# Moving small TensorE work behind the P V bursts, and dealing the score maxima by a table, in a fused attention and mixture-of-experts kernel

## The chip, the cores and the metric

One program on one core of a Trainium2 chip. The metric is device time in microseconds (us). The kernel before has a median of 1517.07 us over 3 runs (1515.82 to 1519.51). The engines of the core work through their own queues in order and wait for one another by semaphores: TensorE (PE in the profile; its weight loads are listed as PEld), VectorE (DVE), ScalarE (ACT), GpSimd (POOL) and SyncE (SP, which issues most DMAs).

## The reference

Attention with pooled queries over 8 batches of 8 heads (1152 keys of 64 values, neighbouring queries averaged to 576), and on its rows a top-1 mixture of 8 experts.

```python
q_pool = q.reshape(B, H, S // 2, 2, D).mean(axis=3)
scores = scale * np.matmul(q_pool, k.transpose(0, 1, 3, 2))
scores = scores - np.max(scores, axis=-1, keepdims=True)
attn = np.exp(scores)
attn = attn / (np.sum(attn, axis=-1, keepdims=True) + 1e-09)
x = np.matmul(attn, v)                       # then rows (batch, query), 512 columns
...
logits = x @ w_gate                          # 8 experts
e_idx = np.argmax(logits, axis=1)
probs = np.exp(logits - logits.max(-1, keepdims=True)); probs /= probs.sum(-1, keepdims=True) + 1e-09
eom = 1.0 / (1.0 + np.exp(-(x @ w_output_gate)))
for e in range(E):
    mask = e_idx == e
    h = np.maximum(x[mask] @ w1[e], 0.0)
    out[mask] = gate_w[mask, None] * eom[mask, e, None] * (h @ w2[e])
```

## The kernel before

**Pairs and steps.** Two heads make a pair; there are 32 pairs, four to a batch. `attention` works in steps, 18 to a pair: one step for each of the 9 blocks of 128 keys of each of the two heads. Below, "step 14" is the place of a step within its pair, counted from 0. The whole order of TensorE, VectorE, ScalarE and GpSimd is the order of the Python loop over `s` (`tc.manual_schedule`, lines 640 to 691); only SyncE's DMAs are ordered by the framework. One step issues, in this order: what was put off in the step before (`sends`, `pendv`), routers, one piece of `fill`, the scores of the step, preparations of later pairs (`prep_at`), maxima, transposes of maxima (`rows`), and a burst of P V.

**Scores** (`scores`, lines 383 to 412). Four matmuls (lines 393 and 395) write one of two score buffers `sps` in PSUM; the buffers alternate from step to step. ScalarE reads it twice, for a high half `ph` in 16 bits and for the full exponent. In the six steps of `PLP` (1, 3, 7, 9, 11 and 13) the second exponent is written back to the PSUM buffer (lines 399 and 400) and VectorE subtracts the two for the low half `pl` (line 403, called `lo`); this subtraction is put off to the start of the next step. In the other twelve steps GpSimd subtracts (line 409).

**Maxima** (`mgen`, lines 308 to 341). The greatest score of each query is found one pair ahead: 27 units to a pair, 9 query tiles by 3 blocks of 384 keys. A unit is two matmuls into a PSUM bank `mp` (line 330; three for tile 4) and one reduction on VectorE (line 331). After 15 units (tiles 0 to 4) and after 27 (tiles 5 to 8) a small reduction (line 338) gathers `m9`. `rows` (lines 360 to 381) transposes it on TensorE (line 365), VectorE splits the result in two (lines 370 and 371, in the next step), and `sends` issues two DMAs from ScalarE's queue into rows 66 and 67 of `qb` (line 376), from which the scores of the next pair subtract it. Up to step `s` the number of units is 1.5 times the steps, rounded down: one in even steps, two in odd ones. From the fourth pair on `rows` is called in even steps, ahead of the burst.

**P V bursts** (`av`, lines 414 to 440). A block of keys is 15 matmuls (lines 424 to 426) of 64 or 65 columns; bursts run in even steps alone, six steps behind the scores, in the sizes of `BURST`. The blocks of one head add up in a single PSUM tile `av`. Its last block is in the burst of step 14 (first head) or step 4 (second head). Then `norm` (lines 433 to 435, VectorE) divides, at the next `pop`, and the next head's burst, in step 16 or 6, overwrites the tile.

**Banks.** `psum` (lines 87 to 101) hands out three PSUM banks in turn, the longest unused first. With `hold` a bank stays out of the turn until `free`. Maxima, their transposes (held until split), the row sums `gmax` of step 14 (line 272, held until `scale(1)`, line 279, at the end of that step), and everything of `logits` and `router` use them.

**Logits and router** (lines 470 to 601). When a pair's rows are done, `logits` transposes them to `xh` and `xl` (line 479, in the starts of steps 8 and 10) and multiplies them by the gate weights in two column ranges of 256 and 320 (line 496, two matmuls each, starts of steps 12 and 14). `wgt` has 128 columns, of which 32 carry weights (`WC`, line 48) and the rest zeros. After a batch's fourth pair the generator goes on with `router`, from step 16: transposes of the logits (line 521), some twenty small VectorE operations on a held bank, then again on another, and five indirect DMAs from GpSimd. A generator that yields 1 goes on in the next even step, one that yields nothing in the next step.

After the attention, `Moe` runs the experts; the change doesn't touch it.

Of the kernel before, what the change touches and what calls it, by code (L numbers as in the profile page):

```python
# [19 lines left out]
LEAD = 18  # L20
L0 = 18
LS = 0
# [6 lines left out]
PREP = ((0, 'lk'), (12, 'kh', 0), (12, 'qsum'), (17, 'kh', 1), (18, 'kl'), (18, 'dk', 0), (19, 'dk', 1), (22, 'qh'), (24, 'dq', 0), (25, 'dq', 1), (26, 'ql'), (29, 'qd'), (30, 'dl', 0), (32, 'dl', 1),  # L29
        (63, 'lv'), (82, 'amax', 0), (88, 'amax', 1), (93, 'gmax'), (94, 'scale', 0), (95, 'scale', 1), (99, 'scale', 2), (100, 'vh', 0), (101, 'vs', 0), (103, 'vl', 0), (107, 'vh', 1), (107, 'vs', 1), (110, 'vl', 1))  # L30
BURST = {0: 2, 2: 2, 4: 2, 6: 2, 8: 1, 10: 2, 12: 2, 14: 2, 16: 3}
PLP = (1, 3, 7, 9, 11, 13)
PLPL = (1, 3, 5, 17)
IMM = 0
# [7 lines left out]
TLAG = 1  # L42
# [2 lines left out]
P32 = 6  # L45
SLEAD = 32
S = 1152
WC = 128
NQ = 576
NC = 9  # L50
SHIFT = 4.0 * math.log(2.0)
# [15 lines left out]
def attention(tc, qT, kT, vL, wg, keep, xrows, idscr, cum, pairs, setup, scat, init, exps):  # L67
    nc = tc.nc
    nb = len(pairs) // 4
    with ExitStack() as ctx:  # L70
# [16 lines left out]
        def psum(hold=False, name="tp"):  # L87

            while len(held) == 3:
                pop() if fill else pendv.pop(0)()  # L90
            k = next(i for i in banks if i not in held)
            free(k)
            if hold:
                held.add(k)
            x = ps_m.tile([128, 512], F32, name=name, tag=f"mp{k}")
            return (x, k) if hold else x

        def free(k):
            held.discard(k)
            banks.remove(k)  # L100
            banks.append(k)
# [22 lines left out]
        def dmaf(o, i, q=nc.sync):  # L124
            q.dma_start(out=o.bitcast(F32), in_=i.bitcast(F32))
# [218 lines left out]
        now = [0]  # L344

        def pop(k=1):
            while k and fill:
                fill.pop(0)()
                k -= 1

        pend_t, pendd = [], []

        def sends():

            while pendd and pendd[0][1] < now[0]:
                pendd.pop(0)[0]()
# [1 line left out]
        pendv = []  # L358

        def rows(force=False):  # L360
            while pend_t and (force or now[0] >= pend_t[0][-1] + TLAG):
                m9, nt, t0, t1, qbf, _ = pend_t.pop(0)
                tp, tk = psum(True)
                tp = tp[0:nt, 0:128]
                nc.tensor.transpose(out=tp, in_=m9[:, 0:nt], identity=ident)
                mr = sm.tile([5, 2, 128], F32R, name="mr")[0:nt]
                c0 = 16.0 * SHIFT

                def split(tp=tp, tk=tk, mr=mr, qbf=qbf, t0=t0, t1=t1, nt=nt):
                    nc.vector.tensor_scalar(out=mr[:, 0], in0=tp, scalar1=c0, scalar2=None, op0=ALU.subtract)  # L370
                    nc.vector.scalar_tensor_tensor(out=mr[:, 1], in0=tp, scalar=c0, in1=mr.bitcast(F32)[:, 0], op0=ALU.subtract, op1=ALU.subtract)
                    free(tk)

                    def send():
                        for j in range(2):
                            dmaf(qbf[66 + j:67 + j, 128 * t0:128 * t1].rearrange("o (t n) -> o t n", n=128), mr[:, j], nc.scalar)
                    pendd.append((send, now[0]))
                if now[0] < 18:
                    split()
                else:  # L380
                    pendv.append(split)

        def scores(st, h):
            ka, kb, qa, qb = st['ka'], st['kb'], st['qa'], st['qb']
            o = h * (NQ + 64)
            for c in range(NC):
# [10 lines left out]
                ph2 = ph.rearrange("p (j n) -> p j n", j=2)  # L397
                if c + 9 * h in (PLP if st['n'] < LASTN else PLPL):
                    nc.scalar.activation(out=ph2, in_=x, func=AF.Exp, scale=1.0 / 16)  # L399
# [42 lines left out]
        routers = []  # L442

        wf = bp.tile([128, 4, 16], F32, name="wf")
        wgt = bp.tile([128, 4, WC], F32R, name="wgt")
        em8 = keep['em8']
# [23 lines left out]
        def logits(b, c, xb):  # L470

            xh = sm.tile([128, NQ], F32R, name="xh", bufs=1)
            xl = sm.tile([128, NQ], F32R, name="xl", bufs=1)
            yield 1
            for c0, c1, grp in ((0, 256, (0, 1)), (256, NQ, (2, 3, 4))):
                tx, tk = psum(True)
                for i, t in enumerate(grp):
                    x = xb[:, t, 128 * c:128 * c + 128]
                    nc.tensor.transpose(out=tx[:, 128 * i:128 * i + 128], in_=x, identity=ident)  # L479
                d = 0  # L480
                for o, w in ((0, c1 - c0),) if c0 == 0 else ((0, 256), (320, 64)):
                    z = slice(c0 + d, c0 + d + w)
                    nc.scalar.copy(out=xh[:, z], in_=tx[:, o:o + w])

                    def sub(o=o, w=w, z=z, tx=tx, tk=tk if not d else None):
                        nc.vector.tensor_tensor(out=xl[:, z], in0=tx[:, o:o + w], in1=xh.bitcast(F32)[:, z], op=ALU.subtract)
                        if tk is not None:
                            free(tk)
                    fill.insert(0, sub)
                    d += w  # L490
                yield 1
            for c0, c1 in ((0, 256), (256, NQ)):
                pop(99)
                tl = psum()
                for j, x in enumerate((xh, xl)):
                    nc.tensor.matmul(tl[:, 0:c1 - c0], lhsT=wgt[:, c], rhs=x[:, c0:c1], start=j == 0, stop=j == 1)  # L496
                if c == 0:
                    nc.vector.tensor_copy(out=lT[:, c0:c1], in_=tl[0:32, 0:c1 - c0])
                else:
                    nc.vector.tensor_tensor(out=lT[:, c0:c1], in0=tl[0:32, 0:c1 - c0], in1=lT[:, c0:c1], op=ALU.add)  # L500
                yield 1
            if c == 3:
                yield from router(b, xb)

# [114 lines left out]
        NP = len(pairs)  # L619
        pos = dict(m=0)  # L620

        def adv(k, g, want):
            while pos[k] < want:
                next(g, None)
                pos[k] += 1
# [3 lines left out]
        def prep_at(s, ph):  # L629
            u = 3 * (s + SLEAD) + ph  # L630
            for n in range(max(u // 54 - 2, 0), min(u // 54 + 2, NP)):
                r = u - 54 * n + min(3 * (LEAD - 15), 2 * n)
                if r == 0:
                    preps[n] = prep(n, PREP if n > 1 else PREP0 if n else PREPF)
                if n in preps:
                    for f in preps[n].pop(r, ()):
                        f()

        E = mybir.EngineType
        with tc.manual_schedule(engines={E.PE, E.DVE, E.Activation, E.Pool}):  # L640
            for s in range(-SLEAD, 0):
                for ph in range(3):
                    prep_at(s, ph)
                if s == -RI:
                    for i in (1, 2):
                        dmaf(QBs[i][64:66], QBs[0][64:66])
                        dmaf(KBs[i][64:68], KBs[0][64:68])
                if s == 1 - SLEAD + INIT:
                    consts()
                if s == -3:  # L650
                    init(0)
                if s >= -int(L0):
                    adv('m', mg, int(1.5 * (s + 1 + L0)))
                    now[0] = s
                    sends()
                    pop(3)
                    rows()
            for s in range(18 * NP + 14):
                now[0] = s
                live = s < 18 * NP  # L660
                if s % 18 == 2 and 0 < s // 18 < 5:
                    with tc.issue_after(lastk[0].ins):
                        init(s // 18)
                sends()
                while pendv:
                    pendv.pop(0)()
                for r in routers:
                    if not s % 2 or not live or not r[1]:
                        r[1] = next(r[0], 0)
                pop()  # L670
                if live:
                    next(sg)
                prep_at(s, 0)
                mw = min(27 * NP, int(1.5 * (s + 1 + min(LEAD, L0 + LS * s))))
                if pos['m'] < mw:
                    adv('m', mg, pos['m'] + 1)
                prep_at(s, 1)
                adv('m', mg, mw)
                if s < 54 or s % 2 == 0:
                    rows()  # L680
                if pos['m'] == 27 * NP:
                    pop(2)
                j = s - ALAG
                for _ in range(BURST.get(j % 18, 0) if 0 <= j < 18 * NP else 0):
                    next(ag)
                prep_at(s, 2)
                if not live:
                    pop(3)
            pop(99)
            for r in routers:  # L690
                for _ in r[0]: pass
# [529 lines left out]
```

## Time and profile before

| | |
|---|---|
| runs, median (lowest to highest) | 1517.07 us (1515.82 to 1519.51) |
| the profiled execution | 1520.83 us, span of its instructions 1519.1 us |
| mean granted TensorE clock | 0.988 |
| DVE busy | 1100.6 us (72%) |
| ACT busy | 1119.0 us (74%) |
| POOL busy | 1014.8 us (67%) |
| attention, by the windows view | from about 26 to 1014 us, TensorE busy 971.3 of 988 us |

A row of the timeline gives the start in us from the span's start, the length in us, the engine, the line and operation, the tiles (out<-in) and the shape. Ends of matmuls are modelled, so the time that one matmul costs is read from its start to the next one's start. In the rows of groups, "x" is the number of instructions, then come their busy time in us and the mean of one in ns, then the engine's idle time just before them. In the waits, the three numbers are the total in us, the number of times, and the longest.

### The profile page before, as it was taken

What the parts mean: (1) busy time and instruction counts of PE and PEld (TensorE: products, weight loads), DVE (VectorE), ACT (ScalarE), POOL (GpSimd) and SP (SyncE); (2) the same over time, 40 slices, a digit from 0 to 9 for tenths busy, and PEclk for the clock granted to TensorE, in tenths of its full rate; (3) what the DMA queues carried; (4) which work ended last, traced back from release to release, by engine and by line L of the source; (5) the groups of instructions that cost most, each with busy time, mean ns of one, the idle gap of its engine ahead of it and who ended that gap; (6) DMA issues with size and microseconds to landing.
All of it is one profiled execution on the core that took longest, in us unless ns stands there. A gap on an engine that the chain in (4) does not pass through costs nothing.

```text
span 1519.1 us, 40914 instructions
## 1 busy us (share of the span) xinstructions
PE 1475.8 (97%) x15838; PEld 1344.3 (88%) x15838; DVE 1100.6 (72%) x2359; ACT 1119.0 (74%) x1949; POOL 1014.8 (67%) x892
## 2 busy tenths in 40 slices
PE   7999999999999999999999999988999999999998
PEld 6999999999998999999999899976888888888875
DVE  7677777777786777777678777737877877777752
ACT  5788888888887878888888888884655655655642
POOL 5887888788878879788888988796243333333410
PEclk9999999999999999999999999998999999999999
DMA  5577466665676556656567556357876676367650
GB/s 169 137 189 191 124 167 166 169 155 134 161 170 159 122 135 172 169 145 163 124 165 180 144 149 167 72 202 270 313 251 236 209 238 238 108 228 256 228 194 36
DMA packets 96787, 265.96 MB, mean 175 GB/s; under 512 B 12906, under 2 KB 17146, under 8 KB 96578
## 3 DMA queue, kind: packets, MB, share of 16 engines
q1 hardware_dynamic: 85994, 241.52, 56.7%
q0 software_dynamic: 9152, 20.85, 3.8%
q8 instruction: 129, 2.11, 0.6%
q10 hardware_dynamic: 1440, 0.89, 0.2%
q14 instruction: 72, 0.59, 0.1%
HBM read 164.23 MB, written 23.02 MB: 123 GB/s over the span
## 4 chain that ended last, share of the span: by engine, by line
PE 91%; DVE 4%; ACT 2%; DMA 1%; issue 1%; POOL 1%; ACTq 0%; POOLq 0%; DVEq 0%; SPq 0%
PE mp L330 20%; PE hps L913 14%; PE sps L393 11%; PE sps L395 9%; PE av L424 6%; PE av L425 6%; PE av L426 6%; PE yp L937 4%; PE yp L935 4%; PE yp L936 4%; DVE pm L331 2%; PE yp L933 1%; PE tp L479 1%; PE xps L892 1%; PE tp L496 1%
## 5 line engine op out<-in xcount | busy, mean ns | idle before, releaser
L331 DVE TENSOR_REDUCE pm<-mp 128x1 f32<-128x384 f32 x864 | 452.9, 550 | 225.4 <-PE mp L330 224.4
L409 POOL TENSOR_TENSOR pl<-p,ph 128x576 f16<-128x576 f32 x386 | 494.2, 1286 | 152.8 <-ACT ph L408 122.2
L407 ACT ACTIVATE p<-sps 128x576 f32<-128x576 f32 x386 | 252.8, 655 | 103.1 <-PE sps L395 61.0
L330 PE MATMUL mp<-ka,qa 128*128 128x384 f32 x960 | 315.5, 345 | 0.0
L424 PEld LDWEIGHTS <-ph 128*128 128x128 f16 x2880 | 263.3, 97 | 39.6 <-issue 28.3
L424 PE MATMUL av<-vt,ph 128*128 128x65 f16 x2880 | 296.8, 194 | 0.0
L425 PE MATMUL av<-vt,ph 128*128 128x64 f16 x2880 | 294.8, 195 | 0.0
L426 PE MATMUL av<-vt,pl 128*128 128x65 f16 x2880 | 293.9, 193 | 0.0
L393 PE MATMUL sps<-qa,ka 128*128 128x288 f32 x1152 | 279.5, 324 | 12.7 <-ACT ph L408 8.7
L425 PEld LDWEIGHTS <-ph 128*128 128x128 f16 x2880 | 266.2, 97 | 0.8
L426 PEld LDWEIGHTS <-pl 128*128 128x128 f16 x2880 | 266.4, 99 | 0.0
L330 PE MATMUL mp<-kb,qb 66*128 66x384 f32 x768 | 261.5, 340 | 0.9 <-DVE kb L204 0.6
L408 ACT ACTIVATE ph<-sps 128x576 f16<-128x576 f32 x386 | 251.4, 651 | 0.0
L395 PE MATMUL sps<-qb,kb 68*128 68x288 f32 x1152 | 248.1, 298 | 0.0
L913 PE MATMUL hps<-x,w1h 128*128 128x512 f32 (+2 forms) x704 | 224.9, 384 | 4.2 <-DVE x L897 4.2
L393 PEld LDWEIGHTS sps<-qa,ka 128*128 128x128 f32 x1152 | 185.2, 192 | 17.3 <-ACT ph L408 11.7
L395 PEld LDWEIGHTS sps<-qb,kb 68*128 68x128 f32 x1152 | 186.9, 191 | 0.0
L330 PEld LDWEIGHTS mp<-ka,qa 128*128 128x128 f32 x960 | 179.4, 191 | 1.7 <-DVE pm L331 1.5
L915 ACT COPY hs<-hps 128x512 f32<-128x512 f32 (+2 forms) x88 | 47.4, 538 | 168.2 <-PE hps L913 168.2
L913 PE MATMUL hps<-x,w1l 128*128 128x256 f32 (+2 forms) x704 | 163.5, 273 | 0.0
L403 DVE TENSOR_TENSOR pl<-sps,ph 128x576 f16<-128x576 f32 x190 | 143.6, 756 | 15.7 <-ACT sps L400 14.0
L399 ACT ACTIVATE ph<-sps 128x576 f16<-128x576 f32 x190 | 124.4, 655 | 40.4 <-PE sps L395 31.3
(254 smaller groups left out, 2944.4 us busy)
## 6 DMA issues: line engine op xcount, KB each, us to landing
ka<-xk SPq DMA_DIRECT2D x120, 288.0 KB
raw1b<-in_w_dram SPq DMA_DIRECT2D x24, 1024.0 KB
raw2b<-in_w_dram SPq DMA_DIRECT2D x24, 1024.0 KB
raw1a<-in_w_dram SPq DMA_DIRECT2D x22, 1024.0 KB
raw2a<-in_w_dram SPq DMA_DIRECT2D x22, 1024.0 KB
vp<-in_vL_dram SPq DMA_DIRECT2D x32, 576.0 KB
qp<-in_qT_dram SPq DMA_DIRECT2D x31, 576.0 KB
kpf<-in_kT_dram SPq DMA_DIRECT2D x31, 576.0 KB
```

Of the source, the lines that this page charges most:

```text
L330: nc.tensor.matmul(mp, lhsT=l, rhs=r, start=j == 0, stop=j == len(ops) - 1)
L331: nc.vector.tensor_reduce(out=pm[:, i:i + 1], in_=mp, axis=AX.X, op=ALU.max)
L393: nc.tensor.matmul(sps[:, j, 0:288], lhsT=ka[:, h, ks], rhs=qa[:, o + 288 * j:o + 288 * j + 288], start=True, stop=False)
L395: nc.tensor.matmul(sps[:, j, 0:288], lhsT=kb[:, h, ks], rhs=qb[:, h, 288 * j:288 * j + 288], start=False, stop=True)
L403: nc.vector.tensor_tensor(out=pl.rearrange("p (j n) -> p j n", j=2), in0=x, in1=ph2, op=ALU.subtract)
L407: nc.scalar.activation(out=p32.rearrange("p (j n) -> p j n", j=2), in_=x, func=AF.Exp, scale=1.0 / 16)
L408: e_ = nc.scalar.activation(out=ph2, in_=x, func=AF.Exp, scale=1.0 / 16)
L409: nc.gpsimd.tensor_tensor(out=pl, in0=p32, in1=ph, op=ALU.subtract)
L424: nc.tensor.matmul(av_[:, qb, 0:65], lhsT=hi, rhs=vt[:, h, c, 0:65], start=c == 0 and qb == 0, stop=False)
L425: nc.tensor.matmul(av_[:, qb, 0:64], lhsT=hi, rhs=vt[:, h, c, 66:130], start=False, stop=False)
L426: nc.tensor.matmul(av_[:, qb, 0:65], lhsT=lo, rhs=vt[:, h, c, 0:65], start=False, stop=c == NC - 1 and qb == 4)
L913: nc.tensor.matmul(hp[:, f, 0:n], lhsT=W1[l][g][:, c, fs], rhs=d['x'][:, c, 0:n], start=c == 0 and l == 0, stop=c == 3 and l == 0)
```

## The change

The maxima of a step come from the table `UNITS` instead of the rule of 1.5. Against the rule one unit moves from step 1 to 0, from 11 to 10, from 13 to 12 and from 15 to 14. Transposes of maxima are made behind the burst of an even step (in the first three pairs they can still come ahead of it); those of tiles 0 to 4 are held back by two steps more, from step 12 to 14. `logits` yields 4 after its second transposes and after its first product; the loop turns 4 into 2 behind the burst of an even step and resumes a 2 behind the burst of the next one. So the two gate products move from the starts of steps 12 and 14 to the ends of steps 12 and 16, and the router begins at step 18, which is step 0 of the pair after, not 16. `wgt` has 32 columns, and the products write 32 partitions.

```diff
+UNITS = (2, 1, 1, 2, 1, 2, 1, 2, 1, 2, 2, 1, 2, 1, 2, 1, 1, 2)
...
-WC = 128
+WC = 32
...
-            while pend_t and (force or now[0] >= pend_t[0][-1] + TLAG):
+            while pend_t and (force or now[0] >= pend_t[0][-1] + (TLAG if pend_t[0][2] or now[0] < 54 else TLAG + 2)):
...
-                yield 1
+                yield 1 if c0 == 0 else 4
...
-                    nc.tensor.matmul(tl[:, 0:c1 - c0], lhsT=wgt[:, c], rhs=x[:, c0:c1], start=j == 0, stop=j == 1)
+                    nc.tensor.matmul(tl[0:32, 0:c1 - c0], lhsT=wgt[:, c], rhs=x[:, c0:c1], start=j == 0, stop=j == 1)
...
-                yield 1
+                yield 4 if c0 == 0 else 1
...
-                    if not s % 2 or not live or not r[1]:
+                    if not live or not r[1] or r[1] == 1 and not s % 2:
                         r[1] = next(r[0], 0)
...
-                mw = min(27 * NP, int(1.5 * (s + 1 + min(LEAD, L0 + LS * s))))
+                mw = min(27 * NP, 27 * (s // 18 + 1) + sum(UNITS[:s % 18 + 1]))
...
-                if s < 54 or s % 2 == 0:
+                if s < 54:
                     rows()
...
                     next(ag)
+                if s % 2 == 0:
+                    rows()
+                    for r in routers:
+                        if r[1] == 2:
+                            r[1] = next(r[0], 0)
+                        elif r[1] == 4:
+                            r[1] = 2
```

## The prediction

> **What bounds the kernel now.** I read the page first, then the waits, then the timelines of one ordinary pair (the sixteenth, whose step 13 starts at 515.44 us), engine by engine.
>
> ```profile
> span 1519.1 us, 40914 instructions
> ...
> PE 1475.8 (97%) x15838; PEld 1344.3 (88%) x15838; DVE 1100.6 (72%) x2359; ACT 1119.0 (74%) x1949; POOL 1014.8 (67%) x892
> ...
> PE mp L330 20%; PE hps L913 14%; PE sps L393 11%; PE sps L395 9%; PE av L424 6%; PE av L425 6%; PE av L426 6%; PE yp L937 4%; PE yp L935 4%; PE yp L936 4%; DVE pm L331 2%; PE yp L933 1%; PE tp L479 1%; PE xps L892 1%; PE tp L496 1%
> ```
>
> The chain that ended last is TensorE's own order of work; what the change moves, L330's maxima, stands at its head, and the gate products (L496) are its 1%. TensorE waits for almost nothing, so whatever it is spared counts in full, and so does every new wait.
>
> ```profile
> PEld sps L393 <- ACT ph L408: 11.7, 13, 2.5
> ...
> PEld tp L479 <- DVE pm L331: 5.1, 9, 0.6
> ```
>
> These are its two old waits that matter: scores that wait for ScalarE to clear a score buffer, and transposes that wait 0.57 us each for a bank that VectorE must clear.
>
> ```profile
> 514.25 0.33 PE L330 MATMUL mp<-kb,qb 66*128 66x384 f32 x1
> 514.43 0.27 PE L365 MATMUL tp<-ident,m 128*5 128x128 f32 x1
> 514.54 0.19 PE L424 MATMUL av<-vt,ph 128*128 128x65 f16 x1
> ```
>
> ```profile
> 515.44 0.51 PE L393 MATMUL sps<-qa,ka 128*128 128x288 f32 x2
> ...
> 516.06 0.34 PE L330 MATMUL mp<-ka,qa 128*128 128x384 f32 x1
> ...
> 516.76 0.31 PE L496 MATMUL tp<-xh,wgt 128*128 128x320 f32 x1
> ...
> 517.06 0.42 PE L393 MATMUL sps<-qa,ka 128*128 128x288 f32 x2
> ...
> 517.59 0.28 PE L272 MATMUL tp<-am,onesf 128*128 128x2 f32 x2
> 517.73 0.42 PE L330 MATMUL mp<-ka,qa 128*128 128x384 f32 x1
> 517.99 0.34 PE L330 MATMUL mp<-kb,qb 66*128 66x384 f32 x1
> 518.17 0.21 PE L424 MATMUL av<-vt,ph 128*128 128x65 f16 x1
> ...
> 518.64 0.51 PE L393 MATMUL sps<-qa,ka 128*128 128x288 f32 x2
> ```
>
> Here every instruction starts as soon as the one before has streamed. Scores take 0.53 us (517.06 to 517.59), 0.61 to 0.62 behind a burst (515.44 to 516.06); their first two matmuls last 0.51 instead of 0.42. A unit of maxima takes 0.35 (516.06 to 516.76 are two), a burst of one block 0.47 (518.17 to 518.64).
>
> **The change part by part.**
>
> *Behind the burst, the gain.* The extra 0.08 us of scores behind a burst is a 128-column weight load that the short P V matmuls do not cover: behind the longer gate products the same scores have no such loss. Anything with a light weight load and a long enough stream, put between burst and scores, gets these 0.08 us for nothing.
>
> ```profile
> L496 PEld LDWEIGHTS tp<-xh,wgt 128*128 128x128 f32 x64 | 12.2, 190 | 1.0 <-DVE pm L331 0.6 <-ACT xh L483 0.4
> ...
> L365 PEld LDWEIGHTS tp<-ident,m 128*5 128x5 f32 x32 | 2.8, 87 | 1.0 <-DVE m L338 0.6 <-DVE ri L786 0.4
> ```
>
> A transpose of maxima loads 5 columns (87 ns against 190). Ahead of the burst it costs 0.11 us (514.43 to 514.54), less some 0.01, as a burst starts a little slower without it: 0.10. Behind the burst it costs its 0.11 less the 0.08 it hides: 0.03. That saves 0.07 each for two in each of 28 pairs and one in the fourth: 57 x 0.07 = 4.0 us. The gate products stream as long as before (0.15 us each here); with the full load of 190 ns they would themselves pay the 0.08 behind a burst and gain nothing. A 32-column load isn't in the trace. Between the two rows by columns it would be 87 + 27/123 x 103 = 110 ns, near the lower one, so I take the whole saving, 62 x 0.08 = 5.0 us (two groups in 31 pairs; the last pair's run after the steps). Its bounds are 0 and 5.0. Together -9.0 us, or -4.0.
>
> [...]
>
> *Fewer zeros by themselves.* A 128-column load was hidden behind the product before it (516.76 to 517.06, two products of 0.15, is the stream alone), so unmoved it would gain nothing. VectorE read only 32 partitions before, too.
>
> *The table.* No unit is added. Steps 0, 10, 12 and 14 get two, the steps after them one: TensorE's sum is the same, but step 13 shrinks, from two units and a product (516.06 to 517.06) to one unit, 0.35. Step 14 now asks for four banks: the row sums hold one to the step's end, two units take the other two, and then the transpose must have the first unit's bank back. What clears it stands behind the subtraction of step 13 in VectorE's queue.
>
> ```profile
> 516.80 0.65 ACT L400 ACTIVATE sps<-sps 128x576 f32<-128x576 f32 x1
> 517.27 0.69 ACTq L125 DMA_DIRECT2D qb<-mr  x1
> ```
>
> ```profile
> 515.56 0.27 DVE L370 TENSOR_SCALAR mr<-tp 5x128 fp32r<-5x128 f32 x1
> 515.86 0.28 DVE L371 SCALAR_TENSOR_TENSOR mr<-tp,mr 5x128 fp32r<-5x128 f32 x1
> ...
> 517.55 0.76 DVE L403 TENSOR_TENSOR pl<-sps,ph 128x576 f16<-128x576 f32 x1
> 518.23 0.47 DVE L500 TENSOR_TENSOR lT<-tp,lT 32x320 f32<-32x320 f32 x1
> 518.63 0.54 DVE L331 TENSOR_REDUCE pm<-mp 128x1 f32<-128x384 f32 x1
> 519.09 0.15 DVE L277 TENSOR_SCALAR tp<-tp 128x2 uint32<-128x2 uint32 x1
> 519.27 0.16 DVE L279 TENSOR_SCALAR inv<-tp 128x2 f32<-128x2 f32 x1
> 519.35 0.21 DVE L433 TENSOR_SCALAR r<-av,sc 128x5 f32<-128x5 f32 x1
> ...
> 519.82 0.49 DVE L435 TENSOR_TENSOR xb<-av,r 128x320 f32<-128x320 f32 x1
> ```
>
> I walk both queues from the end of step 13's scores (516.06 above). VectorE: the subtraction starts at +1.49, when ScalarE's second exponent is out (517.45), and leaves after 0.68; the first unit's reduction ends at 2.17 + 0.54 = +2.71. TensorE: one unit 0.35, scores 0.53, row sums with the slower unit behind them 0.22, two units 0.70, the burst 0.47: it is at the transpose at +2.27. **It waits 0.44 us**, or 0.5 with a semaphore's delay. VectorE goes on: the reduction leaves at +2.63, then `scale` 0.18, the second reduction 0.46, `scale` 0.10, the split 0.30 + 0.27, which the transpose has brought here from a step earlier, and `norm` 0.96 (519.35 to 520.31): +4.90. TensorE without any wait would be at the next head's burst in step 16 at 2.27 + 0.11 + 0.53 + 0.35 + 0.53 + 0.35 = +4.14. That burst overwrites the tile which `norm` reads. So the two waits come to **some 0.8 us a pair**, where there were none: now the burst of step 16 comes at 518.64 + 0.61 + 0.70 + 0.53 + 0.35 = 520.83, 0.5 us after `norm`. If the splits queue tighter it is 0.65, with every semaphore's delay 0.95. In 28 pairs, 22.4 us (18.2 to 26.6); in the first three the transpose can stay ahead, and I leave them at nothing.
>
> *The router, two steps later.* Its banks are held in steps 0 to 4 and 6 to 10 of the next pair instead of two steps less. In step 3 two units then find the bank of the maxima's transpose still unsplit, and in step 10 the second transposes meet the router's second bank. Each is like the collision that the trace has in step 8 (0.57 us, above): 2 x 0.57 in 7 pairs, 8.0 us, between 0 (another bank happens to be free) and 12. VectorE's and GpSimd's router work is otherwise the same.
>
> *The DMAs of the maxima,* two per group on ScalarE's queue, come two steps later for tiles 0 to 4.
>
> ```profile
> 735.86 2.82 ACTq L125 DMA_DIRECT2D qb<-mr  x2
> ```
>
> In this pair ScalarE's queue was held for 2.82 us by the two, where an issue is 0.7: an older transfer on the same semaphore had to land first. That is what the 11.7 us of scores waiting for ScalarE mostly are. Three microseconds later those transfers have landed, unless the framework deals the semaphores another way. I take three quarters, -8.8 us, between -11.7 and 0. Queued behind these issues stand step 16's exponents and the value copies; by the walk they lose 0.5 us and TensorE doesn't notice.
>
> *Sum:* 1520.83 - 9.0 + 22.4 + 8.0 - 8.8 = 1533.4 us for an execution like the profiled one. That one was 3.76 us over the median of the runs, so the median comes to **1529.7 us**. With all low ends together it is 1515, with all high ends 1552; the high ones have separate causes and will hardly meet, so I give this case 1515 to 1546.
>
> **The rivals.**
>
> *Faster: VectorE keeps up.* If in step 14 the reduction isn't behind the subtraction, or ScalarE clears step 13 earlier by the 0.8 us, only the gains are left: 1517.07 - 9.0 - 8.8 = 1499 us. For it speaks that VectorE is busy 72% only and that ScalarE loses a queue wait; it decides where the bank is back before +2.27. Against it stands the exponent's end at +1.39, which moves with the scores themselves: a shorter step 13 brings TensorE to the bank sooner and VectorE not at all.
>
> *No change.* The router's collisions don't come, ScalarE's waits all go, and the pair loses 0.65: 1517.07 - 9.0 + 18.2 - 11.7 = 1515 us.
>
> *Column tiles drain the array.* A change of the array's shape is in the trace, at the transposes of logits with 32 rows:
>
> ```profile
> 423.98 0.33 PE L330 MATMUL mp<-kb,qb 66*128 66x384 f32 x1
> 424.25 0.49 PE L521 MATMUL tp<-ident,lT 32*128 32x32 f32 x5
> 424.67 0.53 PE L393 MATMUL sps<-qa,ka 128*128 128x288 f32 x2
> ```
>
> It starts 0.27 us after the maxima's matmul, not 0.18, and five short transposes and the way out take 0.42: some 0.09 in and 0.2 out. If products of 32 columns did that, 62 groups would lose 0.29 each, 18 us: 1548 us. Against it: transposes with 5 columns (514.43) come and go without a gap. [...]
>
> *The maxima come too late.* Their second DMA is issued at 517.27 in step 14, for the scores of the next pair's step 0. These come one step 15 (1.31 us), one step 16 (1.82) and one step 17 (1.31) after 518.64, at 523.1 by the costs above, so it has 5.8 us now and, two steps (2 x 1.4) later, 3.0. If landing took 4, TensorE would lose 1.0 us in 28 pairs: 1558 us. No row gives its landing; that it moves 2.5 KB speaks against it.
>
> *The table does nothing*, because `mw` is already met: not so, the running sums differ in steps 0, 10, 12 and 14.
>
> **How the numbers follow.** Forecast 0.58 (0.06 of it at its low end, within the bound), faster 0.18, no change 0.12, drain 0.05, late maxima 0.07. A measurement of this kernel can tell 0.3%, 4.6 us. Slower: 0.52 + 0.05 + 0.07 = 0.64; the same: 0.06 + 0.12 = 0.18; faster: 0.18. The likeliest case alone spans 1515 to 1546; the range must reach into the faster one and takes 1508 to 1546, leaving out about 0.10 below and 0.09 above.
>
> **What would show it.** Right: in the waits, rows of L365 for the reductions of L331 and of L424 for L435, each some 28 times and 0.4 us; scores behind a moved transpose or product with 0.42 instead of 0.51; the queue's 2.82 us gone; pairs of some 30.6 us, and TensorE's busy share lower. Wrong: no wait at the transposes of step 14; a gap before L496 of 0.1 us or more (drain); L395 waiting for a DMA in step 0; or a time below 1512 us, which would mean that VectorE's order of step 14 isn't the one I walked.

## The result, and the profile after

After: 1613.35 us median of 6 runs (1609.15 to 1615.17), beside 1516.88 us of 6 runs of the kernel before; the ratio is 1.0628 (95% interval 1.0609 to 1.0647). The change costs 96.5 us. The forecast was slower, by 12.8 us.

The head of the page, with the chain that ended last (line numbers of after are one higher than before up to the burst, later by more):

```profile
span 1613.0 us, 40820 instructions
...
PE 1516.1 (94%) x15838; PEld 1359.7 (84%) x15838; DVE 1109.0 (69%) x2359; ACT 1111.6 (69%) x1949; POOL 1018.3 (63%) x892
...
PE 75%; DMA 10%; DVE 6%; issue 3%; ACT 3%; POOL 2%; SPq 0%; ACTq 0%; POOLq 0%; DVEq 0%
PE mp L331 15%; PE hps L921 14%; PE sps L394 8%; PE sps L396 8%; DMA qb<-mr 8%; PE av L425 5%; PE av L426 4%; PE av L427 4%; PE yp L945 4%; PE yp L943 4%; PE yp L944 4%; DVE pm L332 2%; DVE pl L404 2%; DMA qa<-yq 1%; PE yp L941 1%
```

TensorE's share fell from 97% to 94%, and a transfer that wasn't on the chain at all, the maxima's DMA into `qb`, now holds 8% of it. The waits name who stands behind it (total in us, times, longest):

```profile
PE sps L396 <- DMA qb<-mr: 50.3, 23, 5.1
PE tp L366 <- DVE pm L332: 8.7, 27, 0.4
...
PEld sps L396 <- DMA qb<-mr: 52.8, 22, 5.3
PEld tp L366 <- DVE pm L332: 12.0, 27, 0.5
PEld L425 <- DVE xb L436: 7.1, 29, 0.3
```

The waits of L366 (the transposes of maxima in step 14) and of L425 (the burst of step 16) were forecast; that of L396 (the scores of step 0, for the maxima's DMA) was the rival with a chance of 0.07. Read from each start to the next, it is 54.0 us in 23 pairs: 4.2 to 5.3 us in step 0 of the third pair of a batch (pairs 6, 10, 14, 18, 22 and 26 from 0), 0.7 to 2.2 in 17 others. The timeline shows both kinds, first an ordinary pair (steps 14 to 0), then a third one:

```profile
529.36 0.55 DVE L332 TENSOR_REDUCE pm<-mp 128x1 f32<-128x384 f32 x1
...
529.97 0.28 PE L366 MATMUL tp<-ident,m 128*5 128x128 f32 x1 [0.31 <-DVE pm L332]
...
530.00 0.51 PE L394 MATMUL sps<-qa,ka 128*128 128x288 f32 x2
...
531.67 0.69 ACTq L126 DMA_DIRECT2D qb<-mr  x1
...
532.87 0.31 PE L497 MATMUL tp<-xh,wgt 128*32 128x320 f32 x1
...
533.02 0.31 PE L497 MATMUL tp<-xl,wgt 128*32 128x320 f32 x1
...
533.17 0.43 PE L394 MATMUL sps<-qa,ka 128*128 128x288 f32 x2
...
534.40 0.43 PE L394 MATMUL sps<-qa,ka 128*128 128x288 f32 x2
...
535.60 0.30 PEld L396 LDWEIGHTS sps<-qb,kb 68*128 68x128 f32 x2 [1.00 <-DMA qb<-mr]
...
766.29 0.53 SPq L576 DMA_DIRECT2D xrows<-xb  x1
...
767.36 0.66 SPq L577 DMA_DIRECT2D xrows<-xb  x1
...
768.06 1.52 SPq L152 DMA_DIRECT2D kpf<-in_kT_dram  x1
...
770.18 1.41 ACTq L126 DMA_DIRECT2D qb<-mr  x1
...
778.24 0.82 PE L396 MATMUL sps<-qb,kb 68*128 68x288 f32 x2 [4.83 <-DMA qb<-mr]
```

In step 14 the transpose (529.97) starts when the reduction of 529.36 has cleared its bank. The second DMA is issued at 531.67; the weights of the scores that need it could load at 534.60 (535.60 less the 1.00 us waited): 3.9 us from issue to use, 2.9 on hand. In the third pair, where the same 2.5 KB take 8.0 us, SyncE had issued the batch's rows (1.2 MB, L576 and L577) and the next keys (L152, 0.6 MB) 2.1 to 3.9 us ahead of them. The gate products also show what was hoped for: 0.15 us each (532.87, 533.02, 533.17), no gap ahead, and scores of 0.43 behind them.

What follows such a wait is in the windows view (stretch, length, busy time of PE, PEld, DVE, ACT and POOL, granted clock, DMA share, GB/s):

```profile
773.00:776.60 3.60, 0.41 (x3) 0.18 (x2) 0.93 (x3) 1.57 (x3) 3.58 (x5) 1.00 1.11 194
776.60:780.00 3.40, 1.76 (x6) 1.62 (x6) 0.26 (x1) 0.84 (x2) 0.86 (x1) 0.51 0.19 73
780.00:783.40 3.40, 3.40 (x38) 3.26 (x37) 0.85 (x2) 1.25 (x3) 2.82 (x3) 0.50 0.00 0
783.40:786.80 3.40, 3.40 (x48) 3.23 (x47) 2.56 (x6) 2.71 (x6) 2.73 (x3) 0.99 0.28 66
```

TensorE stands still for most of the first stretch, and in the next two its clock is halved: a second loss, after the wait. The trace has 81.9 us at half clock within the attention, 20.5 before (10.2 us of each are one stretch at its start).

### The profile page after: what moved, and what is told of

Same layout as the page of the kernel before. It is cut to its first block, busy times and chain, and to the rows that moved or that the text cites. A ratio compares the mean times of both kernels' runs of the same rounds, so it can differ in the third digit from the quotient of the medians.

```text
span 1613.0 us, 40820 instructions
## 1 busy us (share of the span) xinstructions
PE 1516.1 (94%) x15838; PEld 1359.7 (84%) x15838; DVE 1109.0 (69%) x2359; ACT 1111.6 (69%) x1949; POOL 1018.3 (63%) x892
## 4 chain that ended last, share of the span: by engine, by line
PE 75%; DMA 10%; DVE 6%; issue 3%; ACT 3%; POOL 2%; SPq 0%; ACTq 0%; POOLq 0%; DVEq 0%
PE mp L331 15%; PE hps L921 14%; PE sps L394 8%; PE sps L396 8%; DMA qb<-mr 8%; PE av L425 5%; PE av L426 4%; PE av L427 4%; PE yp L945 4%; PE yp L943 4%; PE yp L944 4%; DVE pm L332 2%; DVE pl L404 2%; DMA qa<-yq 1%; PE yp L941 1%
## 5 line engine op out<-in xcount | busy, mean ns | idle before, releaser
L332 DVE TENSOR_REDUCE pm<-mp 128x1 f32<-128x384 f32 x864 | 459.2, 552 | 259.9 <-PE mp L331 258.0
L331 PE MATMUL mp<-ka,qa 128*128 128x384 f32 x960 | 322.4, 352 | 2.3 <-DVE ri L794 0.8
L425 PEld LDWEIGHTS <-ph 128*128 128x128 f16 x2880 | 266.5, 98 | 48.5 <-issue 37.2
L425 PE MATMUL av<-vt,ph 128*128 128x65 f16 x2880 | 305.0, 196 | 0.0
L426 PE MATMUL av<-vt,ph 128*128 128x64 f16 x2880 | 302.2, 196 | 0.0
L396 PE MATMUL sps<-qb,kb 68*128 68x288 f32 x1152 | 254.8, 304 | 50.3 <-DMA qb<-mr 50.3
L427 PE MATMUL av<-vt,pl 128*128 128x65 f16 x2880 | 301.3, 195 | 0.0
L427 PEld LDWEIGHTS <-pl 128*128 128x128 f16 x2880 | 270.9, 100 | 0.0
L426 PEld LDWEIGHTS <-ph 128*128 128x128 f16 x2880 | 270.8, 99 | 0.0
L331 PE MATMUL mp<-kb,qb 66*128 66x384 f32 x768 | 266.7, 347 | 0.6 <-DVE kb L205 0.6
L396 PEld LDWEIGHTS sps<-qb,kb 68*128 68x128 f32 x1152 | 191.2, 195 | 55.2 <-DMA qb<-mr 52.8
L394 PEld LDWEIGHTS sps<-qa,ka 128*128 128x128 f32 x1152 | 194.1, 196 | 13.9 <-issue 3.3
L400 ACT ACTIVATE ph<-sps 128x576 f16<-128x576 f32 x190 | 124.6, 656 | 94.1 <-PE sps L396 87.0
```

Source lines behind the costliest of these rows:

```text
L331: nc.tensor.matmul(mp, lhsT=l, rhs=r, start=j == 0, stop=j == len(ops) - 1)
L332: nc.vector.tensor_reduce(out=pm[:, i:i + 1], in_=mp, axis=AX.X, op=ALU.max)
L394: nc.tensor.matmul(sps[:, j, 0:288], lhsT=ka[:, h, ks], rhs=qa[:, o + 288 * j:o + 288 * j + 288], start=True, stop=False)
L396: nc.tensor.matmul(sps[:, j, 0:288], lhsT=kb[:, h, ks], rhs=qb[:, h, 288 * j:288 * j + 288], start=False, stop=True)
L425: nc.tensor.matmul(av_[:, qb, 0:65], lhsT=hi, rhs=vt[:, h, c, 0:65], start=c == 0 and qb == 0, stop=False)
L426: nc.tensor.matmul(av_[:, qb, 0:64], lhsT=hi, rhs=vt[:, h, c, 66:130], start=False, stop=False)
```

## The experiments

Two theories at first. **Late:** the two steps by which the transposes of tiles 0 to 4 are held make their DMAs late. **Table:** the loss is the banks of step 14, with two units dealt there. Runs are medians; the kernel before, run beside them, had 1515.96 to 1519.26 us.

**The hold undone (a_lag), the table undone (a_rule), both (a_lag_rule).**

```diff
# a_lag, a_lag_rule
-  ... pend_t[0][-1] + (TLAG if pend_t[0][2] or now[0] < 54 else TLAG + 2)):
+  ... pend_t[0][-1] + TLAG):
# a_rule, a_lag_rule
-  mw = min(27 * NP, 27 * (s // 18 + 1) + sum(UNITS[:s % 18 + 1]))
+  mw = min(27 * NP, int(1.5 * (s + 1 + min(LEAD, L0 + LS * s))))
```

> The changed kernel, but the transposes of maxima of tiles 0 to 4 are not held back by two steps more (step 12, behind the burst, not 14). Theory 'late': the 54 us in which the scores of step 0 wait for the DMAs of the maxima, and the slower clock after such waits, come from those two steps; they vanish, and with them the 0.48 us wait of the transpose for a bank in step 14, as the row sums hold no bank in step 12. What is left is the table: some 0.2 to 0.3 us a pair above the kernel before, and the router's extra second in every fourth pair: 1520 to 1530 us. Rival 'table': the banks of step 14 and the two units there are the main loss, and the DMA only shows up because of them; the time stays above 1570 us.

> The changed kernel with the old rule for the units (1.5 a step) in place of the table. Theory 'late': the scores of step 0 still wait for the maxima's DMAs in more than 15 pairs, since the transposes still come in step 14; only the 13 us at the transpose of step 14 and some 7 us at the burst of step 16 go: 1575 to 1600 us, with more than 40 us of waits for those DMAs left. Rival 'table': without the table there is nothing to wait for, and the time is below 1530 us.

> Both undone: what is left of the change is the transposes of maxima and the gate products behind the bursts, with 32 weight columns. Both theories agree that the weight load behind a burst is hidden: 9 us less than before, some of it given back in the pair after a batch's last, where the router runs two steps later (0.9 us in 7 pairs): 1508 to 1517 us, the fastest so far. If narrow weights drained the array, it would be above 1530.

Measured: 1544.71, 1593.45 and 1524.48 us (ratios 1.0189, 1.0503 and 1.0048, the last from 1.0030 to 1.0067). So the hold costs 1593.45 - 1524.48 = 69.0 us without the table and 1613.35 - 1544.71 = 68.6 with it; the table costs 20.2 and 19.9. They add up, and 7.5 us are left for the moves alone, where a gain was expected. The second was as expected; the first and the third were misses. In the first the table costs 20 us where 6 to 8 were expected, and that it costs 20 in both pairs of kernels is partly chance: in a_lag step 0's scores wait 2.1 to 2.8 us for the maxima's DMAs in four pairs, 9.9 us in all, in a_lag_rule 1.9 us in one. The third shows that some of the moves lose.

**The row write later on its own queue (a_wr_late).**

```diff
-                if t == 2 and b < nb - 1:
+                if t == 4 and b < nb - 1:
                     wr()
```

> The changed kernel, but a batch's rows are written to memory behind the router's fifth indirect DMA, not behind the third: six steps later, after the maxima of that pair have been sent. Theory 'late, behind the row write': in the six pairs whose wait at step 0 is 4.2 to 5.4 us (the third of each batch of four) the small DMA stands behind the 1.2 MB of the rows, written in the same step; there the wait falls below 2 us, and the time by 20 us or more, clock included. Rival 'late by itself': the landing takes that long whatever else is in flight; these waits stay.

Measured: 1597.75 us in one run, the third pairs still waiting 3.9 to 5.9 us. Inconclusive: SyncE's order is the framework's, and the trace shows the write going out at 757.71, ahead of the maxima's DMAs at 759.56 and 760.37, as it had before.

**The row write on GpSimd's queue (a_wr_pool).** That queue follows the written order.

```diff
+                q = nc.sync if b == nb - 1 else nc.gpsimd
-                nc.sync.dma_start(out=xrows[...], in_=xb[...])    # two of them
+                q.dma_start(out=xrows[...], in_=xb[...])
...
-                if t == 2 and b < nb - 1:
+                if t == 4 and b < nb - 1:
```

> The changed kernel, with the write of the batch's rows (1.2 MB, seven batches) taken from SyncE's queue, where it goes out just ahead of the maxima's DMAs of the second pair, to GpSimd's, behind the fifth indirect DMA, some six steps later. If that write is what makes the third pair of a batch wait 5.0 us rather than 0.7 to 2.2: those seven waits fall to 1 to 2 us and the time to 1580 to 1592 us. If the prefetch of keys beside it is the cause, or the issue alone, they stay at 4 us or more, and the time at 1605 to 1618 us.

Measured: 1587.86 us. Its waits:

```profile
PE sps L396 <- DMA qb<-mr: 19.6, 19, 2.4
```

Of the six third pairs that waited 4.2 to 5.3 us none now waits over 0.9 (0.76, 0.89 and 0.67 in pairs 10, 18 and 26, under 0.3 in the others). So the write, not the prefetch of keys, made these 5 us. The other pairs still wait up to 2.5: there the issue alone is too late. The write hasn't become free: in pairs 7, 11, 15, 19 and 23 the scores of step 0 now wait 1.3 to 3.6 us for ScalarE, 11.9 us in all, for its issue of the maxima's DMAs in step 16 of the pair before stands until an earlier transfer on the same semaphore has landed (251.26 in pair 6, by the trace's record of semaphores; the issue starts at 251.34).

**Lateness alone, in the kernel before (b_send_late).**

```diff
-                    pendd.append((send, now[0]))
+                    pendd.append((send, now[0] + (2 if nt == 5 and now[0] >= 54 else 0)))
```

> The kernel before with one thing changed: the two DMAs of the maxima of tiles 0 to 4 are issued two steps later; transposes, maxima and gate products stay where they were. If the lateness of these DMAs is the loss, it costs what holding the transposes cost (69 us in both pairs of kernels that differ by it): 1575 to 1590 us, with waits of step 0's scores for these DMAs in over 20 pairs, longest (4 to 5 us) in the third pair of a batch. If the held transposes themselves (banks, VectorE's order) are the loss: 1514 to 1525 us.

Measured: 1566.15 us (1.0303 to 1.0354), 50.2 over before: less than expected, but the hold's cost in its main part, with no transposes moved.

```profile
PE sps L395 <- DMA qb<-mr: 35.1, 25, 3.9
```

25 waits appear where there were none. They are shorter than in after, 3.9 us at most: with the router where it was, the larger part of the row write goes out in step 6 (721.72 in the 22nd pair), the DMA in step 16 (738.23). Only 30.7 us are at half clock instead of 81.9.

**The DMAs one step earlier (a_send), and both remedies (a_wr_send).**

```diff
-                    pendd.append((send, now[0]))
+                    if now[0] < 54 or nt == 4:
+                        pendd.append((send, now[0]))
+                    else:
+                        send()
```

> The changed kernel, with the two DMAs of tiles 0 to 4 issued in the step of the split and not in the step after, 1.3 us earlier. If they are late by their issue, each wait of step 0's scores shrinks by some 1.3 us: of 54 us some 25 to 30 are left (0.7 to 2.2 us become 0 to 0.9, 5.0 become 3.7), and fewer windows at half clock: 1570 to 1590 us. If the queue behind other transfers decides when they land, whatever the issue: the waits stay and the time is 1600 to 1615 us. A loss could come from ScalarE, which now waits for VectorE's split ahead of its exponents.

> The changed kernel with both remedies: the row write on GpSimd's queue behind the fifth indirect DMA, and the maxima's DMAs of tiles 0 to 4 issued in the step of the split. If the lateness of these DMAs is all that the hold costs, the scores of step 0 wait under 10 us in all and the time comes to that of the kernel without the hold, 1545 us, plus some 9 us that ScalarE loses by issuing behind the split: 1545 to 1560 us. If the hold costs by itself, 1565 us or more with those waits gone.

Measured: 1590.69 and 1596.24 us. The first is what was expected, 0.7 us over its end, with 28.6 of the 54.0 us of waits left; the second missed by 36 us. Waits of the second:

```profile
PE sps L397 <- ACT ph L412: 28.8, 32, 5.8
...
PE sps L399 <- DMA qb<-mr: 7.5, 9, 2.0
```

```profile
ACT p L411 <- DMA qb<-mr: 27.2, 4, 8.2
```

The waits for the DMAs fell to 7.5 us, but the scores wait 28.8 us for ScalarE. The split isn't the main cause: in each ordinary step 15 ScalarE stands 1.04 us behind VectorE's split ahead of its exponents, but 23.2 of the 28.8 us are six waits of 1.3 to 5.8 us in step 17 of the third pairs of a batch. There ScalarE stands 2.9 to 6.4 us between its last exponent and the issue, in five of the six until an earlier transfer has landed, as in a_wr_pool: in pair 6 the row write had gone out at 238.09 on GpSimd's queue, the last part of the earlier transfer on the issue's semaphore landed at 251.80, and the issue starts at 251.88. The two remedies together only move the wait from step 0's scores to ScalarE's issue. Whether the hold costs anything besides stayed open.

**The DMAs left out altogether (a_nosend; b_nosend in the kernel before).**

```diff
-                    pendd.append((send, now[0]))
+                    if nt == 4 or now[0] < 54:
+                        pendd.append((send, now[0]))
```

> The changed kernel without the two DMAs of the maxima of tiles 0 to 4 from the fourth pair on: rows 66 and 67 of those query columns keep older maxima, so this part of the computation is left out. The hold, the transposes in step 14 and their waits stay. If the lateness of these DMAs is all that the hold costs (69 us), the time comes to 1535 to 1548 us, that of the changed kernel without the hold or a little less. If the hold has a price of its own of some 20 us: 1555 to 1570 us.

> The kernel before, without the same two DMAs (the same part is left out). It prices what these DMAs cost where they are in time: ScalarE's issue and the waits of scores for ScalarE in step 15, which the prediction put at 11.7 us: 1503 to 1508 us. If ScalarE's queue isn't what those waits come from: 1513 to 1518 us.

Measured: 1529.09 us (1.0033 to 1.0094) and 1507.73 us (0.9909 to 0.9956). The hold without its DMAs costs nothing of its own, more clearly than expected: with the 11.5 us that these DMAs cost even in time it would be 1540.6 us, beside 1544.71 without the hold (a_lag). No stretch at half clock is left but the one at the start of the attention. The bank waits of step 14 are all still there:

```profile
PEld tp L366 <- DVE pm L332: 12.0, 27, 0.5
```

So the sum from before to after is: these DMAs cost 11.5 us before (1519.26 - 1507.73) and 84.3 after (1613.35 - 1529.09), 72.7 more; everything else in the change costs 1529.09 - 1507.73 = 21.4 us. (Together 94.1; the kernel before measured 2.4 us more beside these two kernels than beside after.)

**The gate products alone (b_logits)**: `WC` 32, yields and loop of the change, in the kernel before.

> The kernel before with the gate products alone moved behind the bursts of steps 12 and 16, 32 columns wide, and the router with them. By the prediction's price 62 times 0.08 us go, and the router's later start can cost up to 8: 1512 us if the router finds its banks, 1512 to 1520 with its collisions. If a load of 32 columns pays its own way behind a burst: 1517 or more; if it drained TensorE: 1535.

Measured: 1523.50 us (1.0036 to 1.0076), a miss: no gain, 7.5 us lost. Step lengths say why the gain is missing. The products behind the bursts cost 0.08 less, as priced, but steps 11 to 17 of the 14th pair gained only 0.03 us together, for at the end of step 14:

```profile
452.77 0.76 DVE L403 TENSOR_TENSOR pl<-sps,ph 128x576 f16<-128x576 f32 x1
...
453.54 0.19 PE L426 MATMUL av<-vt,pl 128*128 128x65 f16 x1
...
453.68 0.50 PE L393 MATMUL sps<-qa,ka 128*128 128x288 f32 x2
```

The burst's last matmul starts at 453.54 and the scores of step 15 not 0.03 but 0.14 us later: they overwrite the buffer that VectorE's subtraction (452.77 + 0.76 = 453.53) has just left. From the scores of step 13 to those of step 15 the two exponents and the subtraction need 2.93 us (450.75 to 453.68); TensorE took 3.19 before and, without a product in step 13, would take 2.82. The pairs in which the router runs are 0.48 longer (31.47 against 30.99), in 7 pairs 3.4 us. The other 4 us of the loss the traces don't tell: the two profiled executions, 1521.17 and 1520.83 us, hardly differ.

**The transposes alone (b_rows)**: `rows()` behind the burst, no hold, all else as before.

> The kernel before with the transposes of maxima alone moved behind the burst of the same step, none held back. By the prediction 57 x 0.07 = 4.0 us less: 1512 to 1514 us. If VectorE's split or the DMAs, now some 0.9 us later, take it back: 1516 to 1522 us.

Measured: 1516.66 us beside 1518.45 (ratio 0.9966 to 1.0001). By the clock that lies in the range of the rival, and the interval holds both a gain of 3.8 us and none. The step lengths decide: steps 2 and 12 are 0.067 and 0.065 us shorter (medians from the fifth pair on), so the price of 0.07 stands (57 x 0.066 = 3.8 us).

**The table alone (b_table)**: the two lines of `UNITS` and `mw` in the kernel before.

> The kernel before with the table alone. If its two units in steps 10, 12 and 14 by themselves make TensorE wait for banks, it costs the 20 us by which two pairs of kernels with moved transposes and products differ: 1534 to 1540 us. If the table costs only because transposes or products stand behind it: 1515 to 1522 us.

Measured: 1573.44 us (1.0331 to 1.0373): 55 us, far above either expectation.

```profile
PE mp L331 <- DVE lT L501: 16.8, 21, 1.2
PE tp L366 <- DVE lT L501: 13.0, 20, 1.0
```

With the gate products at the starts of steps 12 and 14 and two units behind them, three banks aren't enough: TensorE waits for VectorE's copies of the products. Steps 12 to 15 are 1.86 us longer together, 52 us in 28 pairs. Moving the products behind the bursts takes 35 of these 55 us away again. The parts of the change lean on one another.

**The moves that had met no wait (b_best), and its width (b_best_wide)**: products behind the bursts of steps 12 and 14, transposes of tiles 5 to 8 behind that of step 2; then the same with 128 columns.

```diff
-                yield 4 if c0 == 0 else 1      # of b_logits
+                yield 2 if c0 == 0 else 1
```

> The kernel before with only the moves that the runs so far left a gain for: gate products of 32 columns behind the bursts of steps 12 and 14 (not 16, so the router starts where it did), transposes of tiles 5 to 8 behind the burst of step 2; transposes of tiles 0 to 4, the rule of 1.5 and all DMAs stay. Two products and one transpose save 0.16 and 0.08 us a pair, and steps 13 and 14 together stay longer than the 2.93 us that the score buffer needs: 28 x 0.24 = 6.7 us less, 1509 to 1512 us. If some buffer or bank takes it back, as the scores of step 15 did with the product in step 16: 1514 to 1520 us.

> The same with 128 columns of gate weights as before. By the prediction the full load would pay its own 0.08 us behind a burst: 62 x 0.08 = 5.0 us more than with 32 columns. If the width of the load doesn't matter: the same time within 2 us.

Measured: 1536.03 and 1534.13 us. The first is a miss: 17.6 us lost, by a new wait in step 15, which is 0.76 us longer (21 us in 28 pairs, less what the moves gain):

```profile
PE mp L330 <- DVE lT L500: 12.2, 21, 2.6
```

The product at the end of step 14 takes the bank that step 15's second unit needs, and VectorE comes to it only after the subtraction, a reduction and `norm`. As TensorE waits there anyway, the width of the load shows in no time, and that part of the question isn't answered by the clock. It is by the step lengths: the first product behind a burst took 0.201 and 0.230 us to the next one with 128 columns, 0.121 and 0.150 with 32, the 0.08 that the prediction set.

**Where neither bank nor buffer stands (b_v3)**: b_rows, and the first product (32 columns) behind the burst of step 10; the second stays at the start of step 14.

```diff
-                yield 1
+                yield 1 if c0 == 0 else 2
...
+                if c0 == 0:
+                    yield 1
                 yield 1
```

> The kernel before with the moves left that met no bank and no buffer: transposes of maxima behind the burst of the same step, the first gate product (32 columns) behind the burst of step 10, the second where it was. 0.066 + 0.066 + 0.08 = 0.21 us a pair, 5.9 us in 28 pairs: 1509 to 1513 us. If a bank held by the product in step 11 takes it back: 1516 or more.

Measured: 1510.90 us of 12 runs beside 1516.36 (ratio 0.9973, 0.9958 to 0.9988): as expected, 0.3% faster than the kernel before, and the interval leaves out no change.

```profile
508.46 0.28 PE L496 MATMUL tp<-xh,wgt 128*32 128x256 f32 x1
508.58 0.28 PE L496 MATMUL tp<-xl,wgt 128*32 128x256 f32 x1
508.70 0.43 PE L393 MATMUL sps<-qa,ka 128*128 128x288 f32 x2
```

Two products in 0.24 us, and the scores behind them at 0.43: the load of the first scores is hidden.

## Why the prediction was right in sign and wrong in size

**The step that failed** is the landing of the maxima's DMA, which the sum put at nothing and the rival of the late maxima at a chance of 0.07: "If landing took 4, TensorE would lose 1.0 us in 28 pairs: 1558 us. No row gives its landing; that it moves 2.5 KB speaks against it." The 3.0 us on hand was right (2.9). Landing did take 3.9 in the ordinary pair above, and the size of the transfer doesn't tell it: the same 2.5 KB took 8.0 in the third pair. In the trace of before the packets of this DMA end 1.4 to 3.8 us after its issue, and its semaphore is complete after 1.7 to 5.2 us, over 3.0 in 23 of the 28 pairs; that was there to be counted, against 3.0 us. And of the queues that the DMA is moved past, the step looked at ScalarE's alone. In the second pair of a batch the larger part of the row write was issued in step 6 (691.88 in the 22nd pair), well ahead of the DMA in step 14 (705.19); with the router later it goes out in step 14 (766.29), and the DMA in step 16 comes right behind it: 8.0 us instead of 4. The DMAs' lateness is 73 us in all, where the rival's own price was 28. The forecast has the sign right for another reason than the one that makes most of the time.

**A second loss,** the halved clock after a wait, was in no term. In after, 71.7 us at half clock behind the attention's start (10.2 before) stretched TensorE's work by some 28 us (4 before), an estimate from the longer times from one matmul's start to the next: 10 us within the bursts, 8 at the maxima, 10 at the scores. With the 54.0 us of waits that is 82 of the 84.3 us that the DMAs cost.

**The wait of step 14** was forecast as 0.44 us, 0.5 with a semaphore's delay; it is 0.47 to 0.53 in 27 pairs, 13.0 us. **Step 16's burst** was to wait for `norm` for the rest of the 0.8 us, some 0.36; it waits 0.24 (7.1 us, 29 times). Together 20.1 for the forecast 22.4 us. That the table undone gives back 19.9 is not the same sum: in a_rule the burst still waits 4.4 us for `norm`. By step lengths (medians, after against a_rule) the table costs 11.9 us in steps 14 and 15, 2.5 in step 16, and 5.5 in step 2, which no term had:

```profile
539.70 0.76 DVE L404 TENSOR_TENSOR pl<-sps,ph 128x576 f16<-128x576 f32 x1 [0.39 <-ACT sps L401]
...
540.36 0.27 PE L366 MATMUL tp<-ident,m 128*4 128x128 f32 x1
540.60 0.37 PE L394 MATMUL sps<-qa,ka 128*128 128x288 f32 x1
```

The table makes step 1 shorter (0.97 us in this pair, the sixteenth; 1.32 in a_rule), so TensorE is at the scores of step 3 before VectorE's subtraction has left their buffer (539.70 + 0.76 = 540.46). They start 0.24 us behind the transpose, where 0.03 would do.

**The light loads.** 32 columns load in 108 to 111 ns (medians in b_logits), where 110 was worked out; a transpose behind a burst saves 0.066 (forecast 0.07), a product group 0.08. The products of 32 columns show no gap like that of the rival's 32-row transposes (0.09): the first starts 0.02 to 0.03 us behind the burst's last matmul. What was missed is that a saving on TensorE is kept only if the score buffer and the banks let it: in steps 13 to 15 they don't.

**The router** was to cost 2 x 0.57 us in 7 pairs, 8.0; it cost 0.48 a pair, 3.4 us: in step 10 a wait of 0.34 us, shorter than step 8's, and none in step 3.

**ScalarE's queue:** scores waiting for it (11.7 us) were to lose 8.8; in after the same row is 2.3 us, so 9.4 went. The control without the DMAs prices them at 11.5 us.

So the sum of all but the late DMAs came out near: a_nosend is 9.8 us slower than before (interval 5.0 to 14.3), and the forecast, without the lateness, was 12.8. That is partly luck, since its terms missed in both directions. Of the gain of 5.0 us for the gate products little was kept (b_logits: 0.03 us a pair instead of 0.16), and step 2's 5.5 us were in no term; against that stand the router and the two waits, which cost 4.6 and 2.3 us less than forecast, and the DMAs left out, which take 11.5 us with them instead of 8.8. The moves without hold and table (a_lag_rule) cost 7.5 us where their terms, -9.0 and 8.0, give -1.0; 4 us of that stay unexplained, as in b_logits.

## What to carry to other kernels

When a step is moved, follow its product to its consumer and count the time on hand against the landing of the DMA between them, semaphore and all; here 2.5 KB took 8 us instead of 4 when another queue had issued 1.2 MB of writes 2.8 to 3.9 us and 0.6 MB of keys 2.1 us earlier. Look at the engine that issues, too: here ScalarE's queue stood at an issue (737.99 in before) until an earlier transfer on the DMA's semaphore had landed (737.92). A saving on the busiest engine counts only between two points at which no buffer or bank is due: add up the chain through the other engines for each rotation (here 2.93 us for two score steps) before pricing it, and do it for every step that becomes shorter. Try the parts of a change one at a time, since some cost far more alone (55 us) than together (20).

## What the hardware showed unexpectedly

From its issue to its last packet a DMA of 2.5 KB took 1.4 to 7.5 us in the changed kernel and 1.4 to 3.8 in the kernel before. The six longest, 6.1 to 7.5 us, are those of the third pairs that waited 4.2 to 5.3; the one of 7.2 us, in the 22nd pair, followed a write of 1.2 MB and a load of 0.6 MB from another engine's queue, issued 2.1 to 3.9 us earlier. With the write on GpSimd's queue, and later (a_wr_pool), these waits fell to 0.9 us or less. So the delay goes with that write; how it comes about no run shows.

The issue of such a DMA waited, and ScalarE with it, until the transfer that had last used its semaphore had landed. In the kernel before, the second issue in the prediction's row of 2.82 us starts at 737.99, and the earlier transfer on its semaphore had its last landing at 737.92. In 9 of the pairs 4 to 30 (from 0) both DMAs of the maxima of tiles 0 to 4 were issued so, 0.08 us behind such a landing; the seven waits of scores for ScalarE in step 16 of 0.3 to 2.2 us are all in these nine.

In the changed kernel the stretches at half clock begin at 223.68, 291.95, 326.08, 363.63 us and so on, whole multiples of 3.413 us apart (20, 10 and 11 between these four), and within the attention, its start left out, they last one or two times as long (3.41 or 6.83 us). The six waits of 4.2 to 5.3 us have a stretch of 6.83 each; of the other 17, nine (0.9 to 2.2 us) have one of 3.41 and eight (0.7 to 1.6 us) none. What decides between these no run tells.
